# K by head pairs, V a tile a step: other steps for the transfers of the attention

## The chip, the cores and the metric

The kernel runs on one core of one Trainium2 chip. The metric is the device time of the whole kernel in microseconds (us), as a median of runs: 648.92 before the change (three runs, 647.35 to 651.18). The core has a matrix engine (PE, with its weight loads as PEld), a vector engine (DVE), an engine for activations (ACT), GpSimd (POOL) and SyncE (SP), which here issues most of the transfers between device memory and the core.

## What is computed

Attention over 4 batches, 8 heads, 768 positions and 64 numbers a head: each query sees its neighbours within 16 positions and, beside them, one summary for each of 24 blocks of 32 positions (the maximum of K, the mean of V). Its result, 3072 rows of 512, goes through a mixture of 8 experts, of which the two best are taken for each row.

```
k_sum = k.reshape(B, H, nb, block, D).max(axis=3)
v_sum = v.reshape(B, H, nb, block, D).mean(axis=3)
scores_l = scale * np.matmul(q, k.transpose(0, 1, 3, 2))
scores_s = scale * np.einsum('bhsd,bhnd->bhsn', q, k_sum) + np.log(block)
scores_all = np.concatenate([np.where(mask_l, scores_l, -1e9), scores_s], axis=-1)
out = np.matmul(softmax(scores_all), np.concatenate([v, v_sum], axis=2))
...
logits = x @ w_gate + log1p(exp(x @ w_noise)) * noise
h = np.maximum(x[mask] @ w1[e], 0.0)
out[mask] += top2_w[mask, k, None] * (h @ w2[e])
```

## The kernel before

The attention runs in 24 steps of 128 queries, six to a batch, in one loop over t from -2 to 22 that is pipelined by hand: step t computes the scores of tile t+2 on PE (`scores`, L318), their maximum on DVE (`smax`) and exponentials on ACT (`sexp`), turns the exponentials of tile t+1 (`p_trans`), multiplies tile t with V (`av`, L354), normalizes tile t-1 on DVE (`norm`, L363 to L369) and turns it for the gate (`x_pe`). The gate, the maxima of K, the sums of V and the first expert's w1 are laid between these by a table: `at(t, f, ...)` writes a function down for a time, and `run(t + 0.1)` and the like, at fixed places in the loop's body, call what stands there. So a number in the table sets a place in the program; each engine then works off its own instructions in that order.

Every plain transfer is issued by SP, one after the other. An entry that has to wait, for a buffer that PE or DVE still reads or for a result, holds all behind it. The framework counts the transfers with eight semaphores in turn, so an issue also waits until the eighth transfer before it has landed.

The loads of the attention are these. `load_q` takes a tile of q, 128x512 (L112), into one of five buffers. `load_k` takes half of a batch's K, all four pairs of heads, 128x4x384 (L107); only batch 0 comes by head pairs, 128x768 (L147). `k_piece` reduces K in pieces of 128 positions (L231), `k_head` batch 0 by head pairs (L237). `load_ve` takes a V tile at its place, 128x520 (L143), `v_load` the one that lies 64 positions further, 96x520 (L290). `v_sums` forms the block means of V on PE (L257), which `v_rest` copies into the other V tiles (L280, L283). `x_out` writes 128 finished rows (L373). `w_load` brings an eighth of the first expert's weights (w1 at L731, w2 at L735), `clear` writes zeros to the output (L962). K and V have two buffers, one for even batches and one for odd.

The tables KL, VL, KP, W0, VS and the times of `clear_next` say in which step each comes: of batch b+1, K was asked for in two halves at -1 and 0, at 0 and 2.9, and at 6 and 8.9; three V tiles in step 0 and three in step 1, then two a step; q of step t+5 at the start of step t, and the results of tile t-2 at its end. After the attention come the experts, whose order the change doesn't touch.

Of the kernel before, what the change touches and what calls it, by code (L numbers as in the profile page):

```python
# [8 lines left out]
F32 = mybir.dt.float32  # L9
# [5 lines left out]
OP = mybir.AluOpType  # L15
AX = mybir.AxisListType

B, H, S, D = 4, 8, 768, 64
BLK, WIN = 32, 16
NB = S // BLK  # L20
P = 128
TS = S // P
NT = B * TS
# [5 lines left out]
HP = H // 2  # L29
W = 64 + 2 * WIN  # L30
NK = W + NB
PAD = WIN - 1
# [6 lines left out]
CAP = max(CAPS)  # L39
QN = 3  # L40
QBUF = 5
QA = 5
WARM = 100
SK = HP * NK
SW = 16 * (D + 1)
# [18 lines left out]
def attn_moe(ctx, tc, qt, kt, vt, wgn, noise, w1, w2, out):  # L64
    nc = tc.nc
# [13 lines left out]
    work = ctx.enter_context(tc.tile_pool(name="work", bufs=2, side="right"))  # L79
# [17 lines left out]
    KB, KX = [], []  # L97
# [5 lines left out]
    QT = [keep.tile([P, HP, 2, 64], F32, name=f"q{i}") for i in range(QBUF)]  # L103
    QR = {}

    def load_k(b, j, n=1):
        nc.sync.dma_start(KB[b % 2][:, :, PAD + j * P:PAD + (j + n) * P], kt[b, :, :, j * P:(j + n) * P])  # L107

    def load_q(t):
        QR[t] = QT[t % QBUF]  # L110
        b, j = divmod(t, TS)
        nc.sync.dma_start(QR[t].rearrange("p h b q -> p (h b q)"), qt[b, j])  # L112
# [13 lines left out]
    def kx_sum(t):  # L126
        b, j = divmod(t, TS)
        if j < QN:
            x = KX[t % QN].rearrange("p h b k -> p h (b k)")[:, :, W:W + 2 * NB]
            (nc.gpsimd if b else nc.vector).tensor_copy(x.rearrange("p h (b n) -> p h b n", b=2),  # L130
                                                        KM[b][:, :, None, :].to_broadcast([P, HP, 2, NB]))

    def q_piece(t):
        kx_local(t)
        kx_sum(t)
# [8 lines left out]

    load_q(0)
    for h in range(HP):
        nc.sync.dma_start(KB[0][:, h, PAD:PAD + S], kt[0, :, h])  # L147


    ji = HT[1].rearrange("p f n -> p (f n)").bitcast(I32)[:, SW:SW + P]  # L150
# [73 lines left out]

    KM = {}

    def k_piece(b, j, n=1):
        if j == 0:
            KM[b] = work.tile([P, HP, NB], F32, name="kmax")
        src = KB[b % 2][:, :, PAD + j * P:PAD + (j + n) * P]  # L230
        nc.vector.tensor_reduce(KM[b][:, :, 4 * j:4 * (j + n)],  # L231
                                src.rearrange("p h (n i) -> p h n i", i=BLK), axis=AX.X, op=OP.max)

    def k_head(h):
        if h == 0:
            KM[0] = work.tile([P, HP, NB], F32, name="kmax")
        nc.vector.tensor_reduce(KM[0][:, h], KB[0][:, h, PAD:PAD + S].rearrange("p (n i) -> p n i", i=BLK),  # L237
                                axis=AX.X, op=OP.max)

    VO = []  # L240
# [60 lines left out]
    def mask_sums(t):  # L301
        j = t % TS
        s = SC[t] = gate_space()[:, :, :SK].rearrange("p a (h k) -> p a h k", h=HP)
        for blk in range(2):
            for a in range(2):
                r = slice(64 * a, 64 * a + 64)
                m = masks[1 if (j, blk) == (0, 0) else 2 if (j, blk) == (TS - 1, 1) else 0]
                nc.tensor.matmul(s[64 * blk:64 * blk + 64, a, :, L0[blk]:L0[blk] + W], identb[r, r],
                                 m[r, None, :].to_broadcast([64, HP, W]), start=True, stop=False,
                                 skip_group_check=True)  # L310

    def scores(t):
        s, q, k = SC[t], QR[t], KX[t % QN]
        for hp in range(HP):
            for blk in range(2):
                for a in range(2):
                    d = slice(64 * a, 64 * a + 64)
                    nc.tensor.matmul(s[64 * blk:64 * blk + 64, a, hp, :], q[d, hp, blk], k[d, hp, blk, :], start=False,  # L318
                                     stop=hp == HP - 1, skip_group_check=True)
# [3 lines left out]
    def smax(t):  # L323
        NM[t] = work.tile([P, 2, 2, HP], F32, name="nm", bufs=2)
        nc.vector.tensor_reduce(NM[t][:, 0], SC[t], axis=AX.X, op=OP.max)

    def sexp(t, parts=(0, 1)):
        if 0 in parts:
            PE_[t] = awork.tile([P, 2, HP, NK], F32, name="p")
            nc.scalar.activation(NM[t][:, 1], NM[t][:, 0], AF.Copy, scale=-0.125)  # L330
        for a in parts:
            for hp in range(HP):
                nc.scalar.activation(PE_[t][:, a, hp, :], SC[t][:, a, hp, :], AF.Exp, bias=NM[t][:, 1, a, hp:hp + 1],  # L333
                                     scale=0.125)

    def p_trans(t, a):
        pt = psum.tile([P, HP, P], F32, name="pt", bufs=2)
        for hp in range(HP):
            if t == 0:
                warm_up(1 if a + hp else 8)  # L340
            nc.tensor.transpose(pt[:NK, hp, :], PE_[t][:, a, hp, :], ident)  # L341
        if a == 0:
            PT[t] = awork.tile([P, 2, HP, P], F32, name="pts")
        nc.scalar.activation(PT[t][:NK, a], pt[:NK], AF.Copy)  # L344

    def av_space(t):
        PO[t] = psum.tile([P, 2, 512], F32, name="o")
# [12 lines left out]
    def norm(t, fill=None):  # L360
        o = PO[t][:, :, :4 * (D + 1)].rearrange("p g (h c) -> p g h c", c=D + 1)
        r = work.tile([P, 2, 4], F32, name="r")
        nc.vector.tensor_scalar(r, o[:, :, :, D], 1e-9, 1.0 / XS, op0=OP.add, op1=OP.mult)  # L363
        if fill:
            fill()
        ri = work.tile([P, 2, 4], F32, name="ri")
        nc.vector.reciprocal(ri, r)
        X[t] = work.tile([P, DM], F32, name="x", bufs=5)
        nc.vector.tensor_tensor(X[t].rearrange("p (g h c) -> p g h c", g=2, h=4), o[:, :, :, 0:D],  # L369
                                ri[:, :, :, None].to_broadcast([P, 2, 4, D]), op=OP.mult)  # L370

    def x_out(t):
        xd_w.append(nc.sync.dma_start(xd[t * P:(t + 1) * P], X[t]))  # L373
# [580 lines left out]
    def at(t, f, *a):  # L954
        todo.setdefault(round(t, 3), []).append((f, a))
# [22 lines left out]
    nc.sync.dma_start(noi, noise)  # L978
    load_q(4)
    for h in range(HP):  # L980
        k_head(h)
    q_piece(0)
    q_piece(1)
    at(-0.9, v_sums, 0)
# [2 lines left out]
    w_alloc(0)  # L987
    W0 = [8, 10, 12, 14]
    for i in range(4):
        at(W0[i], w_load, 0, i)  # L990
        for k in range(2):
            at(W0[i] + 3 + k + 0.9, w_part, i, k, 0)
            at(W0[i] + 4 + k + 0.1, w_part, i, k, 1)
    VS = [5, 8, 15]
    KP = [-3, -3, -2, 0, 1, 2]
    KP0 = [1, 1, 2, 2, 3, 3]
    KL = [-6, -6, -6, -3.1, -3.1, -3.1]
    VL = [(0, 0, 0, 1, 1, 1), (4, 4, 5, 5, 6, 6), (10, 10, 11, 11, 12, 13)]
    for b in range(B - 1):
        for j in range(TS):  # L1000
            at((6 * b + KP[j] if b else KP0[j]) + 0.1, k_piece, b + 1, j)
            if j % 3 == 0:
                at(6 * b + KL[j] if b else -1 + j // 3, load_k, b + 1, j, 3)
            at(VL[b][j], load_ve, b + 1, j)
        at(VS[b] + (0.2 if b else -0.1), v_sums, b + 1)
        at(VS[b] + (1.02 if b else 0.5), v_rest, b + 1)
# [6 lines left out]
        at(t, w_part, i, k, 0)  # L1013
    for k in range(2):
        at(22.3, w_part, 4, k, 1)
    for t in (14.8, 16.8, 18.8, 19.8):
        at(t, clear_next)
    at(22.2, gate_b, 4)
    at(22.2, gate_m, 4)
# [35 lines left out]
    def run(t):  # L1055
        for f, a in todo.pop(round(t, 3), []):
            f(*a)
# [3 lines left out]

    mask_sums(0)
    for t in range(-2, NT - 1):
        if QBUF <= t + QA < NT:
            load_q(t + QA)
        u = t + 3
        if t >= 1:
            norm(t - 1, (lambda: kx_sum(u)) if u < NT and u != TS else None)
        run(t + 0.02)
        run(t + 0.03)  # L1070
        if t + 2 < NT:
            scores(t + 2)
        if t == -1:
            q_piece(2)
            q_piece(3)
        run(t + 0.5)
        if t + 2 < NT:
            smax(t + 2)
        if 0 <= t + 1 < NT:
            p_trans(t + 1, 0)  # L1080
            p_trans(t + 1, 1)
        if t + 3 < NT:
            mask_sums(t + 3)
        if t + 2 < NT:
            sexp(t + 2, (0, 1) if t + 3 < NT else (0,))
        if u < NT and t >= 1:
            kx_local(u)
        run(t + 0.1)
        if u == TS:
            kx_sum(u)  # L1090
        run(t + 0.2)
        if t >= 0:
            av_space(t)
        run(t + 0.3)
        run(t + 0.31)
        if t >= 1:
            x_pe(t - 1)
        run(t + 0.4)
        if t >= 1:
            x_copy(t - 1)  # L1100
        if t + 3 == NT:
            sexp(t + 2, (1,))
        if t >= 0:
            av(t)
        run(t)
        run(t + 0.8)
        run(t + 0.9)
        if 0 <= t and t + 3 < NT:
            v_load(t + 3)
        if t >= 2:  # L1110
            x_out(t - 2)

    norm(NT - 2)
    og = psum.tile([P, 2, 512], F32, name="o")
# [28 lines left out]
    spair.close()  # L1143
    banks.append(ctx.enter_context(tc.tile_pool(name="banks", bufs=4, space=PSUM, reuse_waits="tile")))

    for t in range(NT - 3, NT - 1):
        x_out(t)
    low = {}

    def first(f, mid=None):  # L1150
# [338 lines left out]
    for e in range(1, E):  # L1489
# [6 lines left out]
        n = e + 1  # L1496
# [210 lines left out]
```

## Time and profile before

| | us |
|---|---|
| median of three runs | 648.92 |
| profiled execution, its own time | 650.73 |
| profiled execution, span from first to last instruction | 648.9 |
| PE busy | 628.6 (97%) |
| DVE busy | 481.2 (74%) |
| ACT busy | 316.1 (49%) |
| POOL busy | 250.2 (39%) |

The busy time of an engine is the sum of its instructions in the one execution that was profiled. PE is the busiest, so the table alone says little about what the transfers cost: it has to be read by stages, since the attention takes the first 140 us and the experts the rest. "Granted clock" is the share of full speed that PE was given in a stretch.

### The profile page before, as it was taken

The page shows a single profiled execution, that of the slowest core. Times are in us where ns is not written, and L with a number is a line of the kernel's source. Part 1 is how long each engine was busy: PE and PEld are TensorE (multiplying, and loading weights), DVE is VectorE, ACT ScalarE, POOL GpSimd, SP SyncE. Part 2 cuts the span into 40 slices and gives each one's busy share as a digit, 9 for nine tenths or more (in the row PEclk, how much of TensorE's full clock was granted, in tenths as well). Part 3 has the DMA queues.
Part 4 walks back from the last instruction along what each step waited for, and adds up shares of the span by engine and source line. Part 5 has one row for each costly group of instructions (what it writes and reads, how often), then busy time and mean ns, then how long its engine had stood idle before and what let it go on. Part 6 is the DMA issues. An engine that isn't in the chain of part 4 may idle for free.

```text
span 648.9 us, 14149 instructions
## 1 busy us (share of the span) xinstructions
PE 628.6 (97%) x5295; PEld 363.4 (56%) x5295; DVE 481.2 (74%) x1039; ACT 316.1 (49%) x692; POOL 250.2 (39%) x432
## 2 busy tenths in 40 slices
PE   8989898999999999999999999999999999999995
PEld 7778676765554554465446544554454455445542
DVE  5768598979887599368887887988798679767510
ACT  4878597973054354065436433653465256425300
POOL 4352043202335353623572356326632542333041
PEclk9999798999999999999999999999999999999998
DMA  9999978963639595838786688769776868763021
GB/s 304 325 278 342 307 218 275 299 230 124 198 123 252 166 220 144 282 84 170 185 226 172 168 200 246 181 135 225 236 201 136 221 210 165 175 191 123 3 94 51
DMA packets 123709, 127.93 MB, mean 197 GB/s; under 512 B 83242, under 2 KB 86674, under 8 KB 123630
## 3 DMA queue, kind: packets, MB, share of 16 engines
q1 hardware_dynamic: 111838, 90.66, 52.1%
q0 software_dynamic: 11792, 36.27, 18.2%
q8 instruction: 44, 0.72, 0.5%
q14 instruction: 35, 0.29, 0.2%
HBM read 81.85 MB, written 25.61 MB: 166 GB/s over the span
## 4 chain that ended last, share of the span: by engine, by line
PE 86%; DVE 6%; ACT 3%; DMA 2%; issue 2%; SPq 1%; POOL 0%; POOLq 0%; DVEq 0%; ACTq 0%
PE pt L1432 29%; PE h L1360 16%; PE h L854 10%; PE pt L909 7%; PE pt L1360 3%; PE pt L341 3%; PE o L1360 3%; PE s L318 3%; PE o L354 3%; PE h L909 2%; PE o L246 1%; ACT p L333 1%; PE pt L378 1%; DMA vd<-in_vt_dram 1%; DVE y L920 1%
## 5 line engine op out<-in xcount | busy, mean ns | idle before, releaser
L90 POOL DMA_INDIRECT out_dram<-y,tb x52 | 69.5, 1336 | 165.3 <-DVE y L931 127.7
L90 POOL DMA_INDIRECT xg<-xd,tb x54 | 60.9, 1127 | 118.8 <-DVE rh L1388 31.5
L1432 PEld LDWEIGHTS <-hth 128*128 128x128 f16 x576 | 56.3, 98 | 66.7
L931 DVE SCALAR_TENSOR_TENSOR y<-pt,tb,prev 128x512 f32<-128x512 f32 x42 | 31.5, 749 | 64.9 <-PE pt L1432 54.2
L1360 PEld LDWEIGHTS <-w1h 128*128 128x128 f16 x504 | 48.9, 98 | 38.2 <-issue 4.4
L1432 PE MATMUL pt<-w2l,hth 128*128 128x512 f16 x288 | 69.0, 379 | 0.0
L1432 PE MATMUL pt<-w2h,htl 128*128 128x512 f16 x288 | 69.0, 379 | 0.0
L1432 PE MATMUL pt<-w2h,hth 128*128 128x512 f16 x288 | 69.0, 379 | 0.0
L1360 PEld LDWEIGHTS <-w1l 128*128 128x128 f16 x504 | 49.3, 98 | 34.9
L90 POOL DMA_INDIRECT prev<-out_dram,tb x45 | 52.6, 1169 | 23.9 <-issue 13.2
L333 ACT ACTIVATE p<-s,nm 128x120 f32<-128x120 f32 x192 | 51.1, 377 | 0.8
L854 PE MATMUL h<-xte,w1h 128*128 128x384 f16 (+2 forms) x248 | 49.1, 336 | 0.0
L1432 PEld LDWEIGHTS <-htl 128*128 128x128 f16 x288 | 28.2, 98 | 34.0
L1349 ACT ACTIVATE w1h<-stg 128x768 f16<-128x768 f32 (+1 forms) x24 | 22.7, 944 | 40.6 <-DVE stg L1340 40.6
L1392 ACT ACTIVATE hth<-h 128x384 f16<-128x384 f32 (+4 forms) x48 | 23.8, 497 | 35.5 <-PE h L1360 35.5
L1349 ACT ACTIVATE w1l<-stg 128x768 f16<-128x768 f32 (+1 forms) x24 | 22.5, 942 | 37.3 <-DVE stg L1340 37.3
L1360 PE MATMUL h<-xte,w1h 128*128 128x384 f16 (+4 forms) x180 | 39.7, 329 | 0.7 <-DVE h L1386 0.4
L1360 PE MATMUL h<-xte,w1l 128*128 128x384 f16 (+4 forms) x180 | 39.7, 329 | 0.0
L1313 ACT ACTIVATE x<-xt 128x512 f16<-128x512 f32 (+2 forms) x44 | 26.5, 626 | 23.4 <-issue 19.2
L1340 DVE TENSOR_TENSOR stg<-stg 128x256 f32<-128x256 f32 x96 | 36.3, 419 | 0.8
L344 ACT ACTIVATE pts<-pt 120x512 f32<-120x512 f32 x48 | 26.7, 609 | 19.4 <-PE pt L341 19.4
L854 PEld LDWEIGHTS <-w1h 128*128 128x128 f16 x256 | 24.7, 98 | 19.5 <-issue 1.2
(301 smaller groups left out, 1305.7 us busy)
## 6 DMA issues: line engine op xcount, KB each, us to landing
stg<-in_w_dram SPq DMA_DIRECT2D x64, 512.0 KB
q<-in_qt_dram SPq DMA_DIRECT2D x24, 256.0 KB
xd<-x SPq DMA_DIRECT2D x24, 256.0 KB
out_dram<-xg SPq DMA_DIRECT2D x8, 768.0 KB
kb<-in_kt_dram SPq DMA_DIRECT2D x6, 768.0 KB
hth<-in_vt_dram SPq DMA_DIRECT2D x12, 260.0 KB
htl<-in_vt_dram SPq DMA_DIRECT2D x16, 195.0 KB
ve<-in_vt_dram SPq DMA_DIRECT2D x12, 260.0 KB
```

Source lines behind the costliest of these rows:

```text
L90: return nc.gpsimd.indirect_dma_start(**kw)
L333: nc.scalar.activation(PE_[t][:, a, hp, :], SC[t][:, a, hp, :], AF.Exp, bias=NM[t][:, 1, a, hp:hp + 1], scale=0.125)
L344: nc.scalar.activation(PT[t][:NK, a], pt[:NK], AF.Copy)
L854: nc.tensor.matmul(ph[:, :n], w1_of(w, wn, c, f), x[:, xo + c, c0:c1], start=(k == 0), stop=(k == 11))
L909: nc.tensor.matmul(py, hx[:, f, c * P:c * P + P], wv[:, f, :], start=st, stop=sp)
L931: nc.vector.scalar_tensor_tensor(y, py[:, :d], gw, pv[:, :d], op0=OP.mult, op1=OP.add)
L1313: nc.scalar.activation(t[:r, c:c + k], src, AF.Copy)
L1340: nc.vector.tensor_tensor(o, x, y, op=op)
L1349: nc.scalar.activation(hi, x, AF.Copy, scale=W1S)
L1360: nc.tensor.matmul(ph[:, :h], w[:, la, a, P * j:P * j + P], x[:, j, :h], start=start and k == 0, stop=k == 5, skip_group_check=True)
L1392: nc.scalar.activation(hh[:, f, t], src, AF.Relu)
L1432: nc.tensor.matmul(py, x, wv[:, f, :], start=st, stop=sp, skip_group_check=True)
```

## The change

K of batches 1 to 3 is loaded by head pairs, one of four to a step, and reduced by head pairs (`k_head` takes the batch; `k_piece` is gone). V tiles come one to a step, nearly. `load_q` stands after the scores of its step and asks for the tile that goes into the buffer just read, two steps sooner than before. `x_out` writes tile t-1, not t-2, and stands right behind it. The four loads of w1 move from steps 8, 10, 12 and 14 to 7, 12, 13 and 14, and the zeros from 14.8, 16.8, 18.8 and 19.8 to 15.95, 17.95, 19.95 and 20.95.

```diff
-    def load_k(b, j, n=1):
-        nc.sync.dma_start(KB[b % 2][:, :, PAD + j * P:PAD + (j + n) * P], kt[b, :, :, j * P:(j + n) * P])
+    def load_k(b, h):
+        nc.sync.dma_start(KB[b % 2][:, h, PAD:PAD + S], kt[b, :, h])
...
+    def k_head(b, h):
+        if h == 0:
             KM[b] = work.tile([P, HP, NB], F32, name="kmax")
+        nc.vector.tensor_reduce(KM[b][:, h], KB[b % 2][:, h, PAD:PAD + S].rearrange("p (n i) -> p n i", i=BLK),
                                 axis=AX.X, op=OP.max)
...
-        at(W0[i], w_load, 0, i)
+        at((7, 12, 13, 14)[i], w_load, 0, i)
...
-    KP = [-3, -3, -2, 0, 1, 2]
-    KP0 = [1, 1, 2, 2, 3, 3]
-    KL = [-6, -6, -6, -3.1, -3.1, -3.1]
-    VL = [(0, 0, 0, 1, 1, 1), (4, 4, 5, 5, 6, 6), (10, 10, 11, 11, 12, 13)]
+    KL = [(-1.98, -1, 0, 1), (3.95, 4.95, 5.95, 6.95), (8.95, 9.95, 10.95, 11.95)]
+    KP = [(1, 1, 2, 3), (5, 6, 7, 8), (10, 11, 12, 13)]
+    VL = [(-1, 0, 0, 1, 2, 3), (3, 4, 5, 6, 6, 7), (8, 9, 10, 11, 12, 13)]
     for b in range(B - 1):
+        for h in range(HP):
+            at(KL[b][h], load_k, b + 1, h)
+            at(KP[b][h] + 0.1, k_head, b + 1, h)
         for j in range(TS):
-            at((6 * b + KP[j] if b else KP0[j]) + 0.1, k_piece, b + 1, j)
-            if j % 3 == 0:
-                at(6 * b + KL[j] if b else -1 + j // 3, load_k, b + 1, j, 3)
             at(VL[b][j], load_ve, b + 1, j)
...
-    for t in (14.8, 16.8, 18.8, 19.8):
+    for t in (15.95, 17.95, 19.95, 20.95):
         at(t, clear_next)
...
-        if QBUF <= t + QA < NT:
-            load_q(t + QA)
...
+        if t + 2 + QBUF < NT:
+            load_q(t + 2 + QBUF)
+        if t >= 1:
+            x_out(t - 1)
...
-        if t >= 2:
-            x_out(t - 2)
+        run(t + 0.95)
```

PE, ACT and POOL run the same instructions in the same order as before; SP and DVE don't. Steps -1 to 1 stand on SP like this before (a name's number tells its buffer; `hth` and `ve` take V tiles and `hth<-hth` the copies of V's sums, `htl` the V tiles that lie 64 further):

```order
L107 DMA kb_92<-in_kt_dram 128x4x384
L112 DMA q_96<-in_qt_dram 128x512
L143 DMA ve<-in_vt_dram 128x520 x3
L107 DMA kb_92<-in_kt_dram 128x4x384
L107 DMA kb_91<-in_kt_dram 128x4x384
L280 DMA hth<-hth 24x2x520
L290 DMA htl<-in_vt_dram 96x520
L112 DMA q_97<-in_qt_dram 128x512
L143 DMA ve<-in_vt_dram 128x520 x3
L290 DMA htl<-in_vt_dram 96x520
```

The same place on SP now:

```order
L106 DMA kb_92<-in_kt_dram 128x768
L111 DMA q_96<-in_qt_dram 128x512
L111 DMA q_97<-in_qt_dram 128x512
L106 DMA kb_92<-in_kt_dram 128x768
L142 DMA ve<-in_vt_dram 128x520
L111 DMA q_98<-in_qt_dram 128x512
L106 DMA kb_92<-in_kt_dram 128x768
L142 DMA ve<-in_vt_dram 128x520 x2
L272 DMA hth<-hth 24x2x520
L282 DMA htl<-in_vt_dram 96x520
L111 DMA q_99<-in_qt_dram 128x512
L365 DMA xd<-x 128x512
```

The half of batch 2's K (`kb_91`) has left these steps, and two tiles of q and the first results have come in. Steps 13 and 14 on SP before, with w1 (`stg`) and the zeros (`out_dram<-xg`) one behind the other:

```order
L112 DMA q_99<-in_qt_dram 128x512
L143 DMA ve<-in_vt_dram 128x520
L290 DMA htl<-in_vt_dram 96x520
L373 DMA xd<-x 128x512
L112 DMA q_100<-in_qt_dram 128x512
L731 DMA stg<-in_w_dram 128x1024
L962 DMA out_dram<-xg_166 128x3x512
L290 DMA htl<-in_vt_dram 96x520
L373 DMA xd<-x 128x512
```

And steps 13 to 16 on SP now, from the w1 load of step 13 on:

```order
L723 DMA stg<-in_w_dram 128x1024
L142 DMA ve<-in_vt_dram 128x520
L282 DMA htl<-in_vt_dram 96x520
L111 DMA q_97<-in_qt_dram 128x512
L365 DMA xd<-x 128x512
L723 DMA stg<-in_w_dram 128x1024
L282 DMA htl<-in_vt_dram 96x520
L111 DMA q_98<-in_qt_dram 128x512
L365 DMA xd<-x 128x512
L282 DMA vd_102<-in_vt_dram 96x520
L954 DMA out_dram<-xg_166 128x3x512
L272 DMA ve<-ve 24x5x520
```

The two big transfers now stand a step apart, and the zeros directly ahead of the copies of V's sums. Step 7 on SP now has w1 ahead of the last V tile of batch 2 (`hth`), which the V sums of step 8 read:

```order
L111 DMA q_100<-in_qt_dram 128x512
L365 DMA xd<-x 128x512
L723 DMA stg<-in_w_dram 128x1024
L142 DMA hth<-in_vt_dram 128x520
L282 DMA vd_103<-in_vt_dram 96x520
```

Before, that tile was asked for in step 6, and w1 in step 8.

## Rows read from the trace of the kernel before

**Rows 1.** The page's first part: busy us of each engine, its share of the span and its instructions.

```profile
PE 628.6 (97%) x5295; PEld 363.4 (56%) x5295; DVE 481.2 (74%) x1039; ACT 316.1 (49%) x692; POOL 250.2 (39%) x432
```

**Rows 2.** Stretches of 10 us: from:to, length, then busy us (and instructions) of PE, PEld, DVE, ACT and POOL, the granted clock, the share of the DMA engines in use, GB/s.

```profile
60.00:70.00 10.00, 7.51 (x150) 5.89 (x147) 6.15 (x21) 4.29 (x14) 2.47 (x7) 0.91 1.04 293
...
80.00:90.00 10.00, 10.00 (x210) 7.88 (x203) 9.79 (x26) 9.66 (x30) 4.81 (x6) 1.00 0.56 183
90.00:100.00 10.00, 8.19 (x151) 6.18 (x148) 8.73 (x33) 8.35 (x27) 2.98 (x6) 0.95 0.98 319
...
110.00:120.00 10.00, 9.07 (x178) 7.36 (x177) 9.62 (x29) 8.17 (x26) 3.41 (x8) 1.00 1.00 359
...
140.00:150.00 10.00, 10.00 (x94) 6.33 (x93) 8.09 (x50) 4.88 (x13) 0.00 (x0) 1.00 0.93 340
```

**Rows 3.** The same columns for the five longest idle pieces of PE in the attention, each cut from the end of the work before it to the start of the next, and their sum.

```profile
28.20:29.42 1.22, 0.00 (x0) 0.00 (x1) 0.34 (x1) 1.22 (x6) 0.00 (x0) 1.00 1.07 250
40.88:42.51 1.63, 0.00 (x1) 0.00 (x1) 1.56 (x4) 0.00 (x0) 1.22 (x2) 1.00 1.06 352
66.13:68.62 2.49, 0.00 (x0) 0.00 (x1) 0.63 (x1) 0.00 (x0) 0.00 (x0) 0.92 0.98 189
97.13:98.50 1.37, 0.00 (x2) 0.00 (x1) 1.30 (x16) 1.37 (x7) 0.00 (x0) 1.00 1.05 391
111.73:112.66 0.93, 0.01 (x1) 0.00 (x0) 0.90 (x4) 0.83 (x2) 0.69 (x2) 1.00 1.02 377
sum 7.64, PE 0.01 PEld 0.01 DVE 4.74 ACT 3.42 POOL 1.91; mean PE 0.00 PEld 0.00 DVE 0.95 ACT 0.68 POOL 0.38
```

**Rows 4.** From the timeline of PE, the instruction that ends the first of these pieces: start, length, line, form, and in brackets the idle time ahead of it with what ended it ("issue": nothing that the profile shows).

```profile
29.42 0.27 PE L354 MATMUL o<-htl,pts 120*64 120x65 f32 x1 [1.22 <-issue]
```

**Rows 5.** The same columns from the end of one idle piece to the end of another, and for two stretches that end where a piece begins.

```profile
29.40:42.50 13.10, 11.46 (x252) 9.10 (x252) 9.93 (x21) 8.23 (x25) 2.75 (x6) 1.00 0.98 301
42.50:68.60 26.10, 23.62 (x504) 18.89 (x504) 17.80 (x60) 19.49 (x63) 9.76 (x21) 0.99 1.00 298
...
20.90:28.20 7.30, 7.30 (x126) 5.55 (x124) 5.77 (x10) 6.74 (x22) 3.84 (x8) 1.00 1.05 337
60.40:66.10 5.70, 5.70 (x129) 4.56 (x126) 5.01 (x19) 3.90 (x14) 1.53 (x4) 1.00 1.08 344
```

**Rows 6.** The page's third part, the queue of instructions: packets, MB, share of 16 engines' time over the span.

```profile
q8 instruction: 44, 0.72, 0.5%
```

**Rows 7.** The same view of the DMA queues in stretches, in this order: the data queue in 60.4:65.3 (no other queue moved anything), the instruction queue in 65.3:67.1, the data queue in 90.3:96.2 (again alone), and both in 125.4:126.8.

```profile
q1 hardware_dynamic: 970, 1.77, 104.4%
...
q8 instruction: 1, 0.02, 5.4%
...
q1 hardware_dynamic: 733, 1.63, 95.4%
...
q1 hardware_dynamic: 81, 0.13, 25.1%
q8 instruction: 1, 0.02, 4.5%
```

**Rows 8.** Stretches of 2 us behind the third and the fourth piece, columns as in the second group; the granted clock is the third number from the end.

```profile
68.00:70.00 2.00, 1.38 (x14) 1.08 (x15) 0.27 (x1) 0.00 (x0) 0.54 (x2) 0.56 1.01 247
70.00:72.00 2.00, 2.00 (x13) 1.33 (x11) 1.93 (x6) 0.99 (x2) 0.42 (x1) 0.50 1.07 358
72.00:74.00 2.00, 2.00 (x23) 1.67 (x21) 0.57 (x1) 1.97 (x9) 0.00 (x0) 0.50 0.89 295
74.00:76.00 2.00, 2.00 (x56) 1.86 (x52) 0.64 (x4) 1.37 (x5) 0.00 (x0) 0.74 1.01 326
98.00:100.00 2.00, 1.50 (x20) 1.08 (x20) 0.94 (x9) 1.16 (x5) 0.00 (x0) 0.74 1.04 392
100.00:102.00 2.00, 2.00 (x34) 1.81 (x32) 0.63 (x3) 1.39 (x3) 0.00 (x0) 0.50 0.36 134
```

**Rows 9.** From the timeline of SP's queue: start, length, line, transfer and count, at the end of step 0, in step 8 and in step 14.

```profile
18.50 1.88 SPq L107 DMA_DIRECT2D kb<-in_kt_dram  x2
...
56.16 0.82 SPq L731 DMA_DIRECT2D stg<-in_w_dram  x1
57.88 0.59 SPq L107 DMA_DIRECT2D kb<-in_kt_dram  x1
...
89.92 0.48 SPq L731 DMA_DIRECT2D stg<-in_w_dram  x1
90.44 0.52 SPq L962 DMA_DIRECT2D out_dram<-xg  x1
```

**Rows 10.** DVE's two kinds of reduction of K in the first 140 us: shape and count, then busy us, mean ns of one, and idle time ahead with what ended it.

```profile
L231 DVE TENSOR_REDUCE kmax<-kb 128x16 f32<-128x512 f32 x18 | 11.8, 677 | 0.6 <-DMA kb<-in_kt_dram 0.6
L237 DVE TENSOR_REDUCE kmax<-kb 128x24 f32<-128x768 f32 x4 | 3.8, 954 | 2.3 <-DMA kb<-in_kt_dram 2.3
```

**Rows 11.** The page's last part and its longer form: transfers by kind, their number and the KB of each.

```profile
stg<-in_w_dram SPq DMA_DIRECT2D x64, 512.0 KB
...
out_dram<-xg SPq DMA_DIRECT2D x8, 768.0 KB
```

**Rows 12.** From the chain that ended last, in order of time: start, us, what. The V sums of batch 2 on PE, and a V transfer from its issue to its landing.

```profile
56.86 1.46 PE pt L257 x48
...
105.17 7.90 DMA vd<-in_vt_dram
```

## Prediction before the run

> **What bounds the kernel now.** I read the page's busy shares first: PE is busy 628.6 us of the span of 648.9, so all that can be won without touching its work is some 20 us of idle time, and whatever a lowered clock costs [rows 1]. Cut into stretches of 10 us, from 140 us on PE is busy 10.00 of 10 at full clock; the attention ahead of it is where it is not: 7.51 at 60:70, 8.19 at 90:100, 9.07 at 110:120 [rows 2]. The change touches only requests of that part, so the sum is made there, and what is saved there comes off the end, since PE alone sets what follows.
>
> Next, the idle time of PE one piece at a time. Five pieces between 28.2 and 112.7 us add up to 7.64 us [rows 3]. The first is ended by "issue", by nothing that the profile shows, and it stands between two of the 32 equal products of tile t with V (L354), which wait for no one [rows 4]. In the third, ACT and POOL stand still as well [rows 3]: PE is not late for them. From the end of the first piece to that of the second PE ran 252 matmuls with as many weight loads, from there to the end of the third 504, and from 20.9 to the first piece 126 [rows 5]: two blocks, four, one, of 126 each. So the pieces stand at the same place in equal blocks of PE's program. The page has a queue that carries only instructions, 44 packets of 0.72 MB, some 16 KB each; PE's 5,295 matmuls make 42 such blocks [rows 1, 6]. In the block that ends at 66.1, this queue moves nothing from 60.4 to 65.3, while the data queue takes 104.4% of the engines' time; its packet comes at 65.3 to 67.1, and PE, out of instructions at 66.13, goes on at 68.62 [rows 3, 7]. In the block before 97.1 nothing comes from 90.3 to 96.2 either. At 125.4, with data at 25.1%, the packet comes at once [rows 7]. I conclude that PE waits for its own program, whose packets queue behind the data that SP has asked for. A block runs 5.7 to 7.3 us [rows 5], of which the packet and the start take some 3 (65.3 to 68.62); a packet that waits longer than 3 to 4 us shows as idle time.
>
> Two of these pieces cost more than themselves. After 68 us the granted clock is 0.56, 0.50, 0.50, 0.74 in four stretches of 2 us, after 98 us 0.74 and 0.50; that is the lower level, 1.2 GHz, after PE had stood still [rows 8]. The lost share is 2 x (0.44 + 0.50 + 0.50 + 0.26) = 3.4 us, less some 0.3 in which PE still stood: 3.1; and 2 x (0.26 + 0.50) = 1.5 the second time.
>
> **Part by part.** No engine but SP and DVE gets another order. On DVE 18 reductions over 512 columns at 677 ns (12.2 us) become 12 over 768 at 954 ns (11.4 us) [rows 10]: 0.8 us less work, spread over 60 us beside PE's; I take it as nothing. SP issues twelve K transfers in place of six; at 0.6 to 0.9 us each [rows 9] that is at most 6 us more in 100, beside everything else.
>
> What matters is how many KB each step asks for; by its shape a tile of q or results, 128x512 f32, is 256 KB, V 128x520 and 96x520 are 260 and 195, V's sums of batch 0 98, a half of K, 128x4x384, 768, a head pair of it 384; the rest is in [rows 11]. Step 0 asked for q 256, three V tiles 780, two halves of K 1,536, sums 98 and V 195: 2,865 KB; now 256 + 384 + 520 + 98 + 195 = 1,453. Step 8 asked for 256 + 512 (w1) + 768 (K) + 195 + 256 = 1,987; now 1,351. Step 14 asked for 256 + 512 + 768 (zeros) + 195 + 256 = 1,987; now 1,219. The pieces at 28.2, 66.1 and 97.1 belong to blocks that begin right behind these three: K at 18.5 to 20.4, w1 and K at 56.2 to 58.5, w1 and zeros at 89.9 to 91.0 [rows 9]. At some 340 GB/s, as in the block at 60.4 [rows 5], 640 KB less is 1.9 us less queue, 1,400 KB is 4.
>
> - 1.22 us at 28.2: the queue is shorter by up to 4 us, but the two early q loads and the first results take part of it back. Between 0 and 1.22; I keep 0.3.
> - 2.49 at 66.1: 640 KB, 1.9 us less: 0.6 left, with bounds 0 and 2.49.
> - 1.37 at 97.1: the 768 KB of zeros are gone from step 14, 2.3 us: 0.2 left, bounds 0 and 1.37.
> - 1.63 at 40.9: here steps 3 and 4 ask for more than before (V and K together, 1,351 KB in step 4 against 1,227) but without a 768 KB piece: 1.2 left, bounds 0 and 2.5.
> - 0.93 at 111.7: zeros now come at the end of step 15, ahead of the V sums and w2: 0.9 left, bounds 0 and 2.
> - New: w1 now stands in step 7, and the V sums of batch 2 on PE, 1.46 us from 56.86 [rows 12], read in their last eight matmuls a V tile that is asked for behind it in step 7, no longer in step 6. The block that begins near 54.6 also sees these 512 KB. I add 0.8, bounds 0 and 2.5.
>
> The idle pieces go from 7.64 to 0.3 + 0.6 + 0.2 + 1.2 + 0.9 + 0.8 = 4.0: gain 3.6. The pieces of 1.22 and 1.63 left the clock at full [rows 3, 5], so with none over 1.3 the 3.1 us of the slow stretch go too; of the second I count 0.8 of 1.5, as PE then waits for ACT and DVE anyway. After 80 us DVE is busy 9.79, 8.73 and 9.62 of 10 [rows 2], so it becomes late next: of the 2.0 won there (1.2 + 0.8) I give back half, 1.0. Sum: 3.6 + 3.1 + 0.8 - 1.0 = 6.5 us.
>
> The other edits I cost at nothing. q is asked for two steps sooner and now waits on SP for this step's scores; results go a step sooner and wait for DVE's `norm` of this step. Behind them on SP stand this step's V and K. These are wanted a step or more later (about 4 us of PE work), and before the change SP already waited once a step, for PE's last product. If that cover fails, it is the third rival below.
>
> **Trace and notes.** [rows 7] show no instruction packet in 4.9 and 5.9 us with the data queue full. The Trainium skill, page "DMA: Bandwidth & Descriptors", section "Queues, rings and completion order", says that each engine goes round its queues packet by packet, which would let an instruction packet in after one packet of data, however long the line; its page "Runtime: NRT & Kernel Launch", section "Instruction fetch mechanics", calls the crossing of a block "mostly hidden". By these the line's length would not matter and 6.5 would be 0; the trace speaks against it.
>
> **The rivals.** (1) All five pieces go, with both slow stretches: 7.64 + 3.1 + 1.5 = 12.2, so 648.9 - 12.2 = 636.7. For it: the asks of a step now lie between 0.96 and 1.74 MB. Against: the same bytes must move, and 60:66 shows 344 GB/s with the engines full [rows 5]. (2) Nothing is won: the late packets come in other steps, as steps 5, 9, 17 and 19 now ask for 1.7 MB; 648.9, give or take 2. (2b) The packet's wait doesn't depend on the length of the line, but on being one packet among 16 engines that are busy anyway; then smoothing changes nothing: 648.9 as well. This is what the Trainium skill's rule above would give, and [rows 7] leave it little. (3) Slower: PE's V sums at 56.86 wait for the V tile behind w1. The longest wait for a V transfer that the chain shows is 7.90 us [rows 12]. Asked for near 52.4, it would land at 60.3 and is wanted near 58.1: 2.2 us, about as long as the piece that brought the lower clock, so 3.1 more; with nothing won elsewhere 648.9 + 5.3 = 654.2. It decides from a landing later than 5.7 us. Against it: the DMA engines are less full there than around it. That the change does not do what it says is in (2): SP may hold each request until an earlier one has landed, and then the order of asking matters less than the line.
>
> **How the numbers follow.** The profiled run took 650.73 us with a span of 648.9; the median of the runs is 648.92, 1.8 below that run's time. The gain is taken from the median: 648.9 - 6.5 = 642.4. Chances: the forecast (639 to 645.6) 0.50; rival 1 (below 639) 0.12; rival 2 0.24 and 2b 0.04; rival 3 0.10. Faster by over 0.5%, which is 3.2 us and about what a measurement of this kernel can tell from no change: 0.62; within: 0.28; slower: 0.10. The range from 636.5 to 650.5 takes in rival 1 nearly whole and most of rival 2; it leaves out rival 3 and the worse end of 2.
>
> **What would show it.** In the changed profile: the idle pieces at multiples of the block, in sum near 4 us and none above 1.5; the clock at 1.00 from 60 to 80; the end of the attention some 6 us sooner and every stretch after that as before. It is wrong if PE's V sums show a wait for V, if the instruction packets still come over 5 us late, or if DVE's own work takes back all that PE gains after 80 us.

## The result, and the profile after

The changed kernel takes 652.19 us (median of 13 runs, 650.20 to 654.61), the kernel before on the same chip 647.35 (13 runs, 644.66 to 651.61): a ratio of 1.0079, 95% interval 1.0055 to 1.0103. It is slower, by 4.8 us. The forecast was 642.4; the range ended at 650.5, and the sign was wrong.

The profiled execution of the changed kernel took 650.47 us with a span of 648.6. The page's line that answers to [rows 1]:

```profile
PE 625.5 (96%) x5295; PEld 360.8 (56%) x5295; DVE 481.7 (74%) x1033; ACT 316.8 (49%) x692; POOL 250.9 (39%) x432
```

PE's busy time is 3.1 us shorter than in [rows 1], its idle time in the span 2.8 longer (648.6 - 625.5 = 23.1, before 20.3). What it waits for between 5 and 140 us, by the view of waits (us in total, times, the longest):

```profile
PE pt L249 <- DMA hth<-in_vt_dram: 4.2, 1, 4.2
PE pt L333 <- ACT xt L376: 1.4, 3, 0.5
PE o L346 <- DVE lt L398: 1.4, 1, 1.4
PE o L404 <- DVE x L361: 1.3, 2, 0.7
PE pt L333 <- issue: 0.8, 2, 0.7
```

The waits ended by "issue", the late instruction packets of [rows 3], have shrunk to 0.8 us. This part of the theory held. In front of them all stands a wait that the kernel before has not: PE's V sums of batch 2 (L249, before at L257) for a V tile. From the timeline of PE, and from the chain of waits in order of time, the transfer that it waited for, from issue to landing:

```profile
60.10 0.65 PE L249 MATMUL pt<-hth 128*24 128x130 f32 x8 [4.19 <-DMA hth<-in_vt_dram]
```

```profile
52.46 7.59 DMA hth<-in_vt_dram
```

These eight products are the last of 48, those that read the last of the six V tiles. The tile is asked for at 52.46 and PE wants it at 55.9; it lands at 60.05. So its lead, from the asking to the want, is 3.4 us. In the kernel before SP asked for the last two tiles at one place (timeline of SP's queue):

```profile
49.47 0.86 SPq L143 DMA_DIRECT2D hth<-in_vt_dram  x2
```

There the last eight products come near 58.1 [rows 12], some 8 us after the asking, and PE does not wait. What holds the asking in the changed kernel stands ahead of it in the chain:

```profile
46.58 5.87 DMA xd<-x
```

This store of results is the eighth transfer ahead of the tile on SP, and it lands at 52.45: when SP can ask hangs on earlier landings too, and not on the step alone. SP's queue around the asking (start, length, line, transfer):

```profile
51.73 0.33 SPq L723 DMA_DIRECT2D stg<-in_w_dram  x1
52.46 0.33 SPq L142 DMA_DIRECT2D hth<-in_vt_dram  x1
53.48 0.33 SPq L282 DMA_DIRECT2D vd<-in_vt_dram  x1
...
55.97 1.12 SPq L142 DMA_DIRECT2D ve<-in_vt_dram  x1
63.90 0.33 SPq L282 DMA_DIRECT2D htl<-in_vt_dram  x1
64.32 0.64 SPq L106 DMA_DIRECT2D kb<-in_kt_dram  x1
```

SP itself issues nothing from 57.1 to 63.9; its next entry loads into a tile, `htl`, that PE's products with V read. So the DMA engines run empty right after PE's wait, which stretches of 2 us show (columns as in [rows 8]: PE's busy time first, the granted clock third from the end, then the DMA share):

```profile
54.00:56.00 2.00, 1.91 (x48) 1.29 (x46) 1.71 (x3) 1.32 (x4) 0.00 (x0) 1.00 1.07 375
56.00:58.00 2.00, 0.00 (x0) 0.00 (x0) 0.88 (x1) 2.00 (x8) 0.98 (x3) 1.00 1.03 366
58.00:60.00 2.00, 0.00 (x0) 0.00 (x0) 0.00 (x0) 0.04 (x1) 1.46 (x4) 0.93 1.03 333
60.00:62.00 2.00, 1.90 (x19) 1.17 (x21) 1.09 (x4) 0.04 (x1) 0.00 (x0) 0.50 0.26 97
62.00:64.00 2.00, 2.00 (x36) 1.88 (x40) 0.17 (x2) 0.65 (x2) 0.00 (x0) 0.50 0.03 8
64.00:66.00 2.00, 2.00 (x34) 1.70 (x31) 1.26 (x5) 0.00 (x0) 0.24 (x1) 0.50 0.65 131
66.00:68.00 2.00, 2.00 (x36) 1.66 (x38) 1.93 (x10) 1.25 (x4) 1.01 (x3) 0.87 0.76 242
```

PE stands still from 56 to 60, and then runs for six microseconds at 0.50, the lower level of 1.2 GHz: 2 x (0.50 + 0.50 + 0.50 + 0.13) = 3.3 us of clock are gone (the 0.07 that is missing from 58 to 60 falls in PE's standstill). That is rival 3 of the prediction, and a wait of the V sums for V is one of the signs by which it said that it would be wrong.

### The profile page after: what moved, and what is told of

Read it like the earlier page. It is cut to its first block, busy times and chain, and to the rows that moved or that the text cites. A ratio compares the mean times of both kernels' runs of the same rounds, so it can differ in the third digit from the quotient of the medians.

```text
span 648.6 us, 14147 instructions
## 1 busy us (share of the span) xinstructions
PE 625.5 (96%) x5295; PEld 360.8 (56%) x5295; DVE 481.7 (74%) x1033; ACT 316.8 (49%) x692; POOL 250.9 (39%) x432
## 4 chain that ended last, share of the span: by engine, by line
PE 80%; DVE 11%; DMA 4%; issue 2%; ACT 1%; SPq 0%; POOL 0%; POOLq 0%; DVEq 0%; ACTq 0%
PE pt L1423 29%; PE h L1351 16%; PE h L846 10%; PE pt L901 7%; PE pt L1351 3%; PE o L1351 3%; PE h L901 2%; DMA kb<-in_kt_dram 2%; DVE nm L317 2%; PE pt L333 2%; PE o L346 2%; PE s L310 2%; DMA hth<-in_vt_dram 1%; DVE y L912 1%; PE pt L370 1%
## 5 line engine op out<-in xcount | busy, mean ns | idle before, releaser
L89 POOL DMA_INDIRECT xg<-xd,tb x54 | 60.5, 1121 | 119.3 <-DVE dsc L645 32.5
L1386 DVE SCALAR_TENSOR_TENSOR htl<-h,hth 128x384 f16<-128x384 f32 (+4 forms) x48 | 26.4, 563 | 11.8 <-ACT hth L1383 11.5
```

Source lines behind the costliest of these rows:

```text
L89: return nc.gpsimd.indirect_dma_start(**kw)
L1386: nc.vector.scalar_tensor_tensor(hl[:, f, t], src, 0.0, hh[:, f, t], op0=OP.max, op1=OP.subtract)
```

## The experiments

All ratios are to the kernel before, run beside it on the same chip. The clock is the median over a kernel's timed runs of the mean granted clock; "V wait" is the wait of PE's V sums for the V tiles of batch 2 in the one profiled execution. "K later" stands for more time between the asking for K and its sums.

| kernel | V wait, us | clock | ratio | 95% interval |
|---|---|---|---|---|
| changed kernel | 4.2 | 0.993 | 1.0079 | 1.0055 to 1.0103 |
| w1 back in step 8 | 2.6 | 0.993 | 1.0069 | 1.0045 to 1.0094 |
| w1 behind the V tile | 4.1 | 0.992 | 1.0066 | 1.0037 to 1.0095 |
| before, w1 and last V in step 7 | 4.9 | 0.993 | 1.0054 | 1.0031 to 1.0077 |
| changed, K later | 4.4 | 0.992 | 1.0081 | 1.0053 to 1.0108 |
| before, last V in step 7 | 1.9 | 0.997 | 1.0012 | 0.9988 to 1.0036 |
| before, K part alone | 0 | 0.996 | 1.0011 | 0.9991 to 1.0031 |
| before, q and results alone | 0 | 0.997 | 1.0011 | 0.9984 to 1.0038 |
| before, w1 and zeros alone | 0 | 0.996 | 0.9978 | 0.9953 to 1.0003 |
| changed, V sooner, w1 in 8 | 0.5 | 0.997 | 1.0029 | 1.0000 to 1.0057 |
| changed, V sooner, w1 in 8, K later | 0.9 | 0.997 | 0.9993 | 0.9964 to 1.0021 |
| changed, V sooner, K later | 0.5 | 0.998 | 1.0000 | 0.9975 to 1.0026 |
| before, step 0, w1 and zeros | 0 | 0.996 | 1.0039 | 1.0014 to 1.0064 |

The kernel before, run beside the twelve edited ones, has a median clock of 0.996 or 0.997 on each chip.

### Is it w1 in front of the V tile?

The first w1 load is put back into step 8, then only behind the V tile in step 7.

```diff
-        at((7, 12, 13, 14)[i], w_load, 0, i)
+        at((8, 12, 13, 14)[i], w_load, 0, i)
```

> The changed kernel with the first w1 load put back from step 7 to step 8, nothing else. Theory A (the V tile that PE's V sums of batch 2 read stands behind w1 on SP, so PE waits 4.2 us and then loses some 3 us to the lower clock): PE's wait for hth near 56 us falls below 1.5 us, the clock stays at 1.00 from 60 to 66, and the time falls by 4 to 7 us against the changed kernel, to some 0.993 to 1.000 of the kernel before. Theory B (DVE's waits for the head pairs of K are the cost) and theory C (SP is held by its own waits for this step's scores and norm): within 2 us of the changed kernel, 1.005 to 1.010 of the kernel before.

```diff
-        at((7, 12, 13, 14)[i], w_load, 0, i)
+        at((7.8, 12, 13, 14)[i], w_load, 0, i)
```

> The changed kernel with w1 still in step 7, but behind the V tile in place of ahead of it. Theory A: the tile lands 1.5 us sooner (512 KB at some 350 GB/s), PE's wait falls from 4.2 to 2 to 3 us, and the time by 1.5 to 5 us, the more if the clock holds. Theories B and C: no change beyond 2 us.

650.07 us and 649.59: as slow as the changed kernel within the intervals, with V waits of 2.57 and 4.05 us. With w1 out of its way the tile, asked for at 53.73 and 54.72, still let PE go on only at 60.5 and 62.7, 6.8 and 7.9 us later. So w1 alone is not what makes it late: both miss what theory A expected, and stand in the range of theories B and C. Both also show DVE waiting for K in the attention, 4.5 and 7.2 us in sum, and PE behind it: in the first, 2.38 us at 78 on DVE and 2.52 at 80 on PE.

### The same two numbers in the kernel before, and one of them

```diff
-        at(W0[i], w_load, 0, i)
+        at((7, 10, 12, 14)[i], w_load, 0, i)
...
-    VL = [(0, 0, 0, 1, 1, 1), (4, 4, 5, 5, 6, 6), (10, 10, 11, 11, 12, 13)]
+    VL = [(0, 0, 0, 1, 1, 1), (4, 4, 5, 5, 6, 7), (10, 10, 11, 11, 12, 13)]
```

> The kernel before with only this much of the change: the first w1 load in step 7 in place of 8, and the last V tile of batch 2 in step 7 in place of 6, behind it. Theory A: PE waits for that tile near 57 us, and the time is 3 to 8 us above the kernel before (1.005 to 1.012). Theories B and C: within 2 us of it.

649.17 us, 1.0054, at the lower end of theory A's range: two numbers alone bring two thirds of the loss. With the second alone (w1 in step 8 as before):

> The kernel before with one number changed: the last V tile of batch 2 asked for in step 7 in place of 6, and w1 in step 8 as before. Theory A1 (one step between asking and use is too short by itself): TensorE waits 2 to 5 us for the tile at about 58 us, ratio 1.003 to 1.006, as with w1 ahead of it (1.0054). Theory A2 (the prediction's rival: it is the 512 KB of w1 in front of it in the queue): no wait above 1 us, ratio 0.998 to 1.002.

1.0012, between the two theories. From the timelines of PE, first with both numbers, then with V's alone:

```profile
62.38 0.65 PE L257 MATMUL pt<-hth 128*24 128x130 f32 x8 [4.89 <-DMA hth<-in_vt_dram]
```

```profile
60.54 0.42 PE L257 MATMUL pt<-hth 128*24 128x130 f32 x8 [1.85 <-DMA hth<-in_vt_dram]
```

Asked for in step 7, the tile is late in both. With w1 in front it is asked for 3.1 us ahead of PE's want and comes 8.0 us after the asking; without, 4.8 ahead and 6.6 after. So in these two executions the step makes the wait, and w1 in front makes it longer, by about 3 us. The shorter wait was not followed by a lower clock (1.00 in every stretch of 2 us from 56 to 64), and costs too little to be told from nothing.

### K by head pairs alone

> The kernel before with the K part alone: head pairs, one a step, reduced by head pairs in the new steps. Theory B: 3 to 6 us slower than the kernel before (1.005 to 1.010), with DVE waiting for K. Theory A: not slower; 0 to 4 us faster (0.994 to 1.000), since steps 0, 6 and 8 lose a piece of 768 KB and PE's waits for its own program get shorter. Theory C: within 2 us.

The kernel before with the change's `load_k`, `k_head`, KL and KP, everything else as it was: 645.59 us, 1.0011. DVE waits for the head pairs, which are summed about a step after they are asked for (timeline of DVE):

```profile
53.84 0.95 DVE L230 TENSOR_REDUCE kmax<-kb 128x24 f32<-128x768 f32 x1 [2.13 <-DMA kb<-in_kt_dram]
...
73.20 0.95 DVE L230 TENSOR_REDUCE kmax<-kb 128x24 f32<-128x768 f32 x1 [1.07 <-DMA kb<-in_kt_dram]
...
80.33 0.95 DVE L230 TENSOR_REDUCE kmax<-kb 128x24 f32<-128x768 f32 x1 [1.51 <-DMA kb<-in_kt_dram]
```

These are waits that the prediction costed at nothing. By themselves they don't move the time measurably: the ratio is that of theory C, below what B expected of these waits, and above the gain of A.

### Mending V, K, and both

V sooner, then K later, then both. The first and the third also have w1 back in step 8, as above; of K, three head pairs of batch 2 are asked for a step sooner, and most sums stand a step later:

```diff
-    VL = [(-1, 0, 0, 1, 2, 3), (3, 4, 5, 6, 6, 7), (8, 9, 10, 11, 12, 13)]
+    VL = [(-1, 0, 0, 1, 2, 3), (3, 4, 4, 5, 5, 6), (8, 9, 10, 11, 12, 13)]
```

> The changed kernel with the first w1 tile back in step 8 and the V tiles of batch 2 asked for one step sooner for four of the six (steps 3, 4, 4, 5, 5, 6). Theory A (the wait of TensorE's V sums of batch 2 for the last V tile, 4.19 us in the changed kernel, is what turned the gain into a loss): that wait falls below 0.5 us, and with the lower clock behind it some 5 us come back: ratio to the kernel before 0.993 to 1.000. Theory B (VectorE's waits for the K head pairs, 2 to 3 us passed on to TensorE at the gate products, cost as much): the V wait goes, but the K waits stay at 2 us or grow, and the ratio stays at 1.000 to 1.005.

```diff
-    KL = [(-1.98, -1, 0, 1), (3.95, 4.95, 5.95, 6.95), (8.95, 9.95, 10.95, 11.95)]
-    KP = [(1, 1, 2, 3), (5, 6, 7, 8), (10, 11, 12, 13)]
+    KL = [(-1.98, -1, 0, 1), (3.95, 3.95, 4.95, 5.95), (8.95, 9.95, 10.95, 11.95)]
+    KP = [(1, 2, 3, 3), (6, 7, 8, 8), (11, 12, 13, 14)]
```

> The changed kernel with its w1 and V steps kept, and the K head pairs reduced later behind their asking (steps 3.95, 3.95, 4.95, 5.95 for the asking of batch 2, sums in steps 1, 2, 3, 3 and 6, 7, 8, 8 and 11, 12, 13, 14). Theory A: VectorE's waits for K go, the V wait at 58 us stays at 4 us: ratio 1.003 to 1.007. Theory B: the K waits were the larger part: ratio 0.996 to 1.002.

> Both edits, V sooner and K sums later. Theories A and B together (the shorter waits for instructions are a true gain of some 6 us, and the two new waits for data gave it back): no wait of TensorE for V or of VectorE for K above 0.5 us, idle pieces for instructions below 2 us in sum, ratio 0.990 to 0.997. Theory C (the loss comes from SP's own order, the q loads and results asked for at other places): ratio 1.001 to 1.007 as before the edits.

V sooner: 646.14 us, the V wait 0.47, the clock back at 0.997; the ratio of 1.0029 is in the range of theory B and above that of A. K later alone: 650.04, nothing gained, above both ranges and nearer that of theory A. Both: 644.15, slower than the 0.990 to 0.997 expected of A and B together, faster than theory C. These three ran on one chip. Between the second and the third stand V's tiles (and w1 in step 8): 5.9 us of the medians. Between the first and the third stand K's steps: 2.0 us, a ratio of 0.997 of their means (0.995 to 1.000, by drawing the runs anew), barely to be told from nothing. DVE's wait for K between 10 and 140 us, in the first and in the third:

```profile
DVE kmax L229 <- DMA kb<-in_kt_dram: 4.9, 3, 3.1
...
DVE kmax L229 <- DMA kb<-in_kt_dram: 0.2, 1, 0.2
```

So V's wait is the large part, and K's is a small one. In the changed kernel itself DVE waits only 0.8 us for K, so K later alone had little to win there. That V's wait always covers K's is not shown: with w1 behind the V tile both stand side by side, 4.1 and 7.2 us.

> The changed kernel with V sooner and K sums later as in the run of both edits, and w1 in step 7 as the change has it. If V's and K's lead is the whole cause, it is as fast as with w1 in step 8: 0.997 to 1.002. If w1 in step 7 costs by itself: 1.003 or more.

The same with w1 in step 7, as the change has it: 1.0000. This kernel differs from the one with K later alone by the steps of V's tiles and by nothing else. The wait for V's tiles in the one and in the other:

```profile
PE pt L249 <- DMA hth<-in_vt_dram: 4.4, 2, 4.1
...
PE pt L249 <- DMA hth<-in_vt_dram: 0.5, 1, 0.5
```

The ratio falls with it from 1.0081 to 1.0000, each against the kernel before on its own chip. The leads of V and K make up all of the loss that can be measured; with V's tiles sooner, w1's step costs nothing that can be.

### q and results alone, w1 and zeros alone

> The kernel before with one part of the change alone: the q load asked for behind the scores and the results of the step before stored right behind it. Theory C: SP waits for the scores and for the norm of the results ahead of its other transfers, ratio 1.003 to 1.008. Theories A and B: no new wait of TensorE or VectorE, ratio 0.997 to 1.002.

```diff
-        if QBUF <= t + QA < NT:
-            load_q(t + QA)
...
+        if t + 2 + QBUF < NT:
+            load_q(t + 2 + QBUF)
+        if t >= 1:
+            x_out(t - 1)
...
-        if t >= 2:
-            x_out(t - 2)
```

> The kernel before with the w1 loads in steps 7, 12, 13, 14 and the zeros a step later, nothing else. Both theories: the transfers have cover enough, no wait of TensorE for data; ratio 0.996 to 1.001. A ratio above 1.003 would say that w1 and zeros carry a part of the loss, which neither theory has.

```diff
-        at(W0[i], w_load, 0, i)
+        at((7, 12, 13, 14)[i], w_load, 0, i)
...
-    for t in (14.8, 16.8, 18.8, 19.8):
+    for t in (15.95, 17.95, 19.95, 20.95):
```

1.0011 and 0.9978, neither to be told from 1, though the second nearly is. SP's own waits in its new order cost nothing that shows: theory C falls, the more as the mended kernels above have this order too. w1 in step 7 does no harm while V's last tile is asked for in step 6. One wait for data came against the expectation: in the second of the two kernels PE waits 0.96 us at 32.4 for a V tile of the shifted kind (`htl`).

### Where is the gain?

Mended, the kernel is only as fast as before. A second profiled execution of the unchanged kernel before:

> The kernel before once more, unchanged, for a second profiled execution of it. If the profile that the prediction was drawn from is typical: TensorE idle at five places for instructions, some 7.6 us in sum, and mean granted clock about 0.989. If that execution was one with more waiting than most (66 other executions show a mean clock of 0.993 to 0.998): idle of 3 to 5 us in sum at these places, mean clock of 0.995 or more, span 641 to 645 us, and the gain that could be had is at most half of the one predicted.

Its span is 644.5 us with a clock of 0.995, where the first had 648.9 and 0.989: the second of the two expectations. PE's waits between 5 and 140 us, those ended by "issue" and the longest other one:

```profile
PE pt L257 <- issue: 1.8, 1, 1.8
PE pt L341 <- issue: 1.5, 1, 1.5
PE o L354 <- DVE lt L406: 1.5, 1, 1.5
PE o L354 <- issue: 1.0, 1, 1.0
...
PE s L318 <- issue: 0.2, 1, 0.2
```

4.5 us end with "issue"; by the same view the first execution has 6.7. The longest piece of [rows 3] (2.49 us at 66.1) and the stretch at half clock behind it [rows 8] are absent from this one; the stretches are full (columns as in [rows 2]):

```profile
60.00:65.00 5.00, 5.00 (x124) 4.07 (x118) 4.54 (x17) 3.80 (x12) 1.40 (x4) 1.00 1.04 326
65.00:70.00 5.00, 5.00 (x106) 4.02 (x97) 4.82 (x13) 3.83 (x13) 0.96 (x2) 1.00 0.95 262
```

And of the 113 timed executions of the kernel before that stood beside the experiments, none shows a clock below 0.990, and 78 show 0.996 or more (the 0.993 to 0.998 of the expectation leaves out a few). The one that the sum was read from, at 0.989, lay outside them.

The last run keeps only those parts that shorten the asks and leave every transfer of batches 2 and 3 as early as before:

```diff
-    VL = [(0, 0, 0, 1, 1, 1), (4, 4, 5, 5, 6, 6), (10, 10, 11, 11, 12, 13)]
+    VL = [(-1, 0, 0, 1, 2, 3), (4, 4, 5, 5, 6, 6), (10, 10, 11, 11, 12, 13)]
...
+        for h in range(HP if b == 0 else 0):
+            at((-1.98, -1, 0, 1)[h], load_kh, 1, h)
+            at((1, 2, 3, 3)[h] + 0.1, k_head, h, 1)
```

(with w1 and zeros as in the run of these alone)

> The kernel before with only those parts of the change that leave no transfer of batch 2 or 3 later than before: step 0 smoothed (V of batch 1 in steps -1, 0, 0, 1, 2, 3, K of batch 1 by head pairs, its sums in steps 1, 2, 3, 3), w1 in steps 7, 12, 13, 14, zeros a step later; V of batch 2 and K of batches 2 and 3 as before. Theory D (the gain predicted is there, and only the late V and K hide it): no wait of TensorE for V, idle time for instructions below 2.5 us where the second profile of the kernel before has 4.5, ratio 0.990 to 0.996. Theory E (it was mis-sized by the one execution that it was read from): ratio 0.996 to 1.001.

648.64 us, 1.0039: neither theory, slower. "Issue" is down to 2.4 us, but K of batch 1 is late in its turn. From the timelines of DVE and of PE:

```profile
34.35 0.95 DVE L240 TENSOR_REDUCE kmax<-kb 128x24 f32<-128x768 f32 x1 [2.17 <-DMA kb<-in_kt_dram]
```

```profile
35.78 0.95 PE L321 MATMUL s<-kx,q 64*64 64x120 f32 x28 [2.52 <-POOL kx L133]
```

DVE waits for a head pair, POOL copies the maxima into `kx` after it, and the scores on PE wait for POOL. Behind these 2.52 us the granted clock is 0.73, 0.50 and 0.92 in the three stretches of 2 us from 36 to 42, which takes another 2 x (0.27 + 0.50 + 0.08) = 1.7 us. Theory D is not borne out: with no V wait at all, the smoothed step 0 still pays for the shorter line with a later K.

## Why the prediction was wrong

**What bounds the kernel: right in kind.** The runs fit PE's idle pieces hanging on its instruction packets behind SP's data. With smaller asks the waits ended by "issue" are 0.8 us in the changed kernel and 2.1 and 1.1 in the two mended ones (both edits, w1 in step 8 and in step 7), against 4.5 and 6.7 in the two executions of the kernel before, and 3.1 to 3.8 in the three runs that changed only the V tile's step, this and w1's, or the place of q and results. Rival 2b said that they would not change; these rows speak against it. The Trainium skill (page "DMA: Bandwidth & Descriptors", section "Queues, rings and completion order") says that each DMA engine goes round its queues packet by packet. Read as the prediction read it, so that the length of the line would not matter, this does not fit these rows. The fifth piece of [rows 3], 0.93 us at 111.7, is no such wait by the trace: it is ended by POOL's `kx`. The sum kept 0.9 of it, so the gain does not hang on it.

**The failed step: "These are wanted a step or more later (about 4 us of PE work)", and rival 3 at 0.10.** The prediction has the last V tile of batch 2 in two places: under these words at nothing, and as the new term of the idle pieces at 0.8, with bounds 0 and 2.5. PE waited 4.19 us. A step is too short a lead. The landings asked for between 51 and 56 us, in this kernel and the edited ones, took 5.5 to 8.0 us from the asking. I had the figure for it, 7.90 us in [rows 12], and put against it that the DMA engines would be less full there; the trace after shows 1.07, 1.03 and 1.03 from 54 to 60. Rival 3 itself had this wait. I let PE want the tile at 58.1; it wanted it at 55.9, partly because the shorter waits ahead bring PE there sooner (the V sums start at 54.60, before at 56.86), and so waited 4.19 us instead of 2.2. The clock was put at 3.1 and came to 3.3. What it named as the cause, w1 in front of the tile, was not enough: with w1 back in step 8 the ratio is still 1.0069. And that its ratio, 654.2 / 648.92 = 1.008, is the one measured (1.0079) is in part luck: its wait was 2 us too short, and it had nothing won elsewhere, which was not so. Still, it should have been the forecast: the change moved the asking a step later, and the length of a landing stood in the rows.

**"I take it as nothing": the K reductions.** I counted their work and not when their data are there. DVE's waits for K between 10 and 140 us are 4.7 us with the K part alone and 4.9 with V mended; freed of them, the kernel with V mended gains 2.0 us of the medians, at the edge of what can be told.

**The gain of 6.5 us: three terms mis-sized.** The idle pieces (3.6 us won) and the clock (3.9 won) were read from an execution with 7.64 us of pieces and, by [rows 8], two slow stretches. In the second execution of the same kernel the view of waits gives 4.5 us, and one slow stretch, 0.56 and 0.58 at 92 to 96, 1.7 us. The third term is what I gave back, 1.0 us, and it was too small. The sums of all waits of PE that the view lists between 5 and 140 us help here:

| | issue | V | all others | sum |
|---|---|---|---|---|
| before, second execution | 4.5 | 0 | 4.3 | 8.8 |
| changed | 0.8 | 4.2 | 7.4 | 12.4 |
| changed, V sooner, K later | 1.1 | 0.5 | 7.9 | 9.5 |
| the same, w1 in step 8 | 2.1 | 0.9 | 5.4 | 8.4 |

What "issue" loses, the others take. Lines of the mended kernel of the third row:

```profile
PE s L310 <- ACT kx L121: 1.0, 1, 1.0
PE pt L370 <- ACT pts L336: 0.9, 2, 0.6
PE o L404 <- DVE x L361: 0.7, 2, 0.5
PE o L346 <- issue: 0.7, 1, 0.7
...
PE s L310 <- POOL kx L129: 0.5, 1, 0.5
```

There PE waits 1.5 us for `kx` from ACT and POOL, and more than before for DVE's `x` and ACT's exponentials. 3.4 us less of the one and 3.6 more of the other: in this kernel this, not 1.0, is what was given back. In the fourth row it is 2.4 us less and 1.1 more, with 0.9 for V. That PE's late program hid these waits, and did not add to them, fits the rows but is not shown by a run of its own; it rests on one profiled execution of each kernel. The medians agree with it: 0.9993 and 1.0000, with intervals that allow at most 0.4% of gain.

**The account of the loss.** Against the second execution of the kernel before, the changed kernel has 4.2 us of V wait and 3.1 of other waits more, 3.7 of "issue" less, and 3.3 - 1.7 = 1.6 more of lost clock: 5.2 us. The first product of the first expert starts at 138.58 us, 4.7 later than there (133.85), and the medians of the two kernels differ by 4.8. In the first execution it starts at 139.17, later than in the changed kernel: that execution alone would have hidden the loss.

**What stays open.** How much of the 3.1 us of other waits in the changed kernel goes back to K was not parted; and whether some schedule with shorter asks and leads of over 8 us for K is faster than the kernel before was not found. The best measured, w1 and zeros alone, is at 0.9978 with an interval that takes in 1.

## What to carry to other kernels

Where transfers are spread over steps to shorten the queue, hold each one's lead, from its asking to its first use, against the longest landings that the trace shows under that load (here 5.5 to 8 us, with a step of about 4), and not against a step; take the earlier time at which its user would arrive if the change works. Before a sum is made from idle pieces of one execution, see whether its time and mean clock are typical of the kernel's runs, and count on the next engine's waits to appear in the idle time that is taken away.

## What the runs showed that was not expected

The same kernel's idle pieces come and go between executions: of five pieces in [rows 3], the second execution has three (0.96, 1.54 and 1.81 us, at 28.0, 40.4 and 90.5) and not the 2.49 at 66.1. A standstill of PE of nearly one length was followed by a lower clock in one case and not in another: 0.56 and 0.58 behind 1.81 us at 90.5 in the second execution of the kernel before, 1.00 throughout behind 1.85 us at 58.7 with the V tile alone in step 7; and 0.73 and 0.50 behind 2.52 us at 33.3 in the last run, 1.00 behind 2.52 us at 79.6 with w1 back in step 8. And while PE waited for the V tile in the changed kernel, SP came to a stop too. The transfers already asked for filled the DMA engines up to 60 us, and then the share fell from 1.03 to 0.03 within 4 us: nothing new was asked for during the wait, and the next transfers started late.
